# A fused recurrence and long convolution on one core: a list scheduler inside the kernel, the spectral sum on GpSimd, and the recurrence spread into the output stage

## The chip, the cores and the metric

One core of a Trainium2 chip. Times are device microseconds (us) of whole executions. "Span" is the profiled part of one execution, about 1.7 us less in each run here. PE is the tensor engine, PEld its weight loads, DVE the vector engine, ACT the scalar engine, POOL is GpSimd, SP the engine that issues loads and stores.

## The reference, cut to what matters

```python
# x, f_logit: (4, 6272, 256); four independent batches
f = lower_bound + (1 - lower_bound) * sigmoid(f_logit)
h[t] = f[t] * h[t-1] + (1 - f[t]) * x[t]          # recurrence over 6272 steps
x1, x2, x3 = split(h @ w_proj, 3)                  # 256 -> 768
conv = irfft(rfft(x2) * rfft(filter_fft))          # circular, length 6272
out = (x1 * conv * x3) @ w_out
```

Both kernels do the transform as matmuls (6272 = 49 x 128). Each batch passes through these stages: **recurrence** (transposes, a scan on DVE, gate products z = x1 x3), **projection and transform** of x2 (called P and f1), 16 **units** (forward transform, product with the filter's spectrum H, inverse transform), and **output** (last step of the inverse, product with z, projection with w_out).

## The kernel before

It weaves generators in program order. The recurrence of the next batch runs beside the units of this one; output, P and f1 follow alone.

```python
for b in range(B):
    mini(b)
    if b + 1 < B:
        weave((units(b), NU), (hgrn(b + 1), NCHK))
    else:
        run(units(b))
    if b + 1 < B:
        wraps()                    # copies of h that the projection of b+1 reads
    run(phase_o(b))
    if b + 1 < B:
        run(phase_p(b + 1)); run(phase_f1(b + 1))
```

A unit has two DVE products and, for each of four pairs, four inverse matmuls that also do the spectral sum in PSUM:

```python
for o, terms in (...):                                # two forward halves
    ...                                               # 2 matmuls each
    nc.vector.tensor_tensor(P[:TB, o, :, :, 1:64], px..., hh, op=AOP.mult)
for pr in range(UE // 2):
    for n, (a, h, v) in enumerate(((0, 0, VA), (0, 1, VB), (1, 0, VB), (1, 1, VN))):
        nc.tensor.matmul(o, P[:TB, a, h, 2*pr:2*pr+2, :], v[:TB], start=(n == 0), stop=(n == 3))
```

The output takes its PSUM pairs in turn from all eight banks (`pair()`), four pairs in rotation.

Of the kernel before, what the change touches and what calls it, by code (L numbers as in the profile page):

```python
# [9 lines left out]
F32 = mybir.dt.float32  # L10
# [11 lines left out]
S = 6272  # L22
# [4 lines left out]
CH = 512  # L27
NCHK = 13
# [20 lines left out]
def run(gen):  # L49
    for _ in gen:  # L50
        pass


def weave(*gens):

    lists = [(g, n) for g, n in gens]
    done = [0] * len(lists)
    total = sum(n for _, n in lists)
    for _ in range(total):
        k = min((i for i in range(len(lists)) if done[i] < lists[i][1]),  # L60
                key=lambda i: (done[i] + 1) / lists[i][1])
        next(lists[k][0])
        done[k] += 1
    for g, _ in lists:
        run(g)
# [3 lines left out]
def kernel(  # L69
# [13 lines left out]

    konst = ctx.enter_context(tc.tile_pool(name="konst", bufs=1))
    iden = konst.tile([128, 128], F32, name="iden")
    make_identity(nc, iden)
    pi_col = konst.tile([128, 1], F32, name="pi_col")
    nc.vector.memset(pi_col, math.pi)
# [7 lines left out]
    VN = konst.tile([128, 196], F16, name="VN")  # L96
# [9 lines left out]
    HB = (0, S + EW)  # L106

    raws = [HA[:, S + 4096 * k:S + 4096 * (k + 1)].bitcast(F32)
            .rearrange("m (r d) -> m r d", d=D) for k in range(3)]
    hws = [HA[:, S + 12288 + 1024 * k:S + 12288 + 1024 * (k + 1)]  # L110
           .rearrange("p (a n) -> p a n", a=2) for k in range(4)]

    hg = ctx.enter_context(tc.tile_pool(name="hg", bufs=2))
    dram = ctx.enter_context(tc.tile_pool(name="dram", bufs=1, space=bass.MemoryType.DRAM))
    H = [dram.tile([TB, 2, UE * 64], F16, name=f"H{u}") for u in range(NU)]
    zt = [konst.tile([128, 2, S], F16, name="z0"), None]
    psp = ctx.enter_context(tc.tile_pool(name="psp", bufs=1, space=PSUM))
    PS = psp.tile([128, 8, 512], F32, name="PS")
    turn = [0, 2]

    def pair():

        turn[0] = (turn[0] + 1) % turn[1]
        return PS[:, 2 * turn[0]:2 * turn[0] + 2]


    def hgrn(b):
        z = zt[b % 2]
        last = [None, None]
        for c in range(NCHK):  # L130
            t0 = c * CH
            nb = min(CH, S - t0) // 128
            n = nb * 128
            xt = hg.tile([128, 4, D], F32, name="xt", tag="xt", bufs=3)
            nc.sync.dma_start(xt[:, 0:nb], x[b, t0:t0 + n, :].rearrange("(j p) d -> p j d", p=128))
            ft = hg.tile([128, 4, D], F32, name="ft", tag="ft", bufs=3)
            nc.sync.dma_start(ft[:, 0:nb], f_logit[b, t0:t0 + n, :]
                              .rearrange("(j p) d -> p j d", p=128))
            nc.scalar.activation(ft[:, 0:nb], ft[:, 0:nb], AF.Sigmoid, scale=-1.0)  # L139
            nc.gpsimd.tensor_tensor(xt[:, 0:nb], xt[:, 0:nb], ft[:, 0:nb], op=AOP.mult)  # L140
            for kh in range(2):
                cols = slice(kh * 128, kh * 128 + 128)
                sT = PS[:, 6, 0:n]
                uT = PS[:, 7, 0:n]
                for j in range(nb):
                    nc.tensor.transpose(sT[:, j * 128:(j + 1) * 128], ft[:, j, cols], iden[:])  # L146
                for j in range(nb):
                    nc.tensor.transpose(uT[:, j * 128:(j + 1) * 128], xt[:, j, cols], iden[:])  # L148
                fT = hg.tile([128, CH], F32, name="fT", tag="fT")
                nc.scalar.activation(fT[:, 0:n], sT, AF.Identity,  # L150
                                     scale=nomc[:, kh:kh + 1], bias=1.0)
                h = hg.tile([128, CH], F32R, name="h", tag=f"h{kh}")
                nc.vector.tensor_tensor_scan(  # L153
                    h[:, 0:n], fT[:, 0:n], uT,
                    0.0 if c == 0 else last[kh][:, CH - 1:CH].bitcast(F32),
                    op0=AOP.mult, op1=AOP.add)
                last[kh] = h
                nc.gpsimd.tensor_copy(HA[:, HB[kh] + t0:HB[kh] + t0 + n],  # L158
                                      h[:, 0:n].bitcast(F32))
            for jb in range(2):  # L160
                for i in range(2):
                    js = slice(i * 256 + jb * 128, i * 256 + jb * 128 + 128)
                    for kh in range(2):
                        nc.tensor.matmul(PS[:, 4 + i, 0:n], W13[:, kh, js], last[kh][:, 0:n],  # L164
                                         start=(kh == 0), stop=(kh == 1))
                x1s = hg.tile([128, CH], F32, name="x1s", tag="x1s")
                nc.scalar.activation(x1s[:, 0:n], PS[:, 4, 0:n], AF.Copy, scale=ZS)  # L167
                nc.vector.tensor_tensor(z[:, jb, t0:t0 + n], PS[:, 5, 0:n], x1s[:, 0:n],  # L168
                                        op=AOP.mult)
            yield  # L170

    def wraps():
        for a, z in ((0, 2048), (2048, 4096), (4096, E0)):
            nc.sync.dma_start(HA[:, S + a:S + z], HA[:, a:z])
        for a, z in ((128, 2048), (2048, 4096), (4096, S)):
            nc.sync.dma_start(HA[:, HB[1] - S + a:HB[1] - S + z], HA[:, HB[1] + a:HB[1] + z])


    def prepare(tmp):
        wcol = tmp.tile([128, 2], F32, name="wcol")  # L180
        nc.sync.dma_start(wcol, lower_bound.rearrange("(a p) -> p a", p=128))
        nc.vector.tensor_scalar(omc[:], in0=wcol[:], scalar1=-1.0, scalar2=1.0,
                                op0=AOP.mult, op1=AOP.add)
        nc.vector.tensor_scalar(nomc[:], in0=wcol[:], scalar1=1.0, scalar2=-1.0,
                                op0=AOP.mult, op1=AOP.add)


        wp = raws[0][:, 0:6].rearrange("p a d -> p (a d)").rearrange("p (k j) -> p k j", k=2)
        nc.sync.dma_start(wp, moe_w_proj.rearrange("(a p) j -> p a j", p=128))
        wo = raws[1][:, 0:2]  # L190
        nc.sync.dma_start(wo, moe_w_out.rearrange("(a p) j -> p a j", p=128))
        for kh in range(2):
            nc.vector.tensor_scalar(wp[:, kh, :], in0=wp[:, kh, :], scalar1=omc[:, kh:kh + 1],
                                    scalar2=None, op0=AOP.mult)
            for i, j0 in enumerate((0, 512)):
                dst = slice(i * 256, (i + 1) * 256)
                nc.vector.tensor_copy(W13[:, kh, dst], wp[:, kh, j0:j0 + 256])
            for p in range(2):
                nc.vector.tensor_copy(
                    W2[:, kh].rearrange("k (g p e) -> k p e g", p=2, e=2)[:, p],  # L200
                    wp[:, kh, 256 + p * 128:256 + (p + 1) * 128]
                    .rearrange("k (e g) -> k e g", e=2))
        nc.vector.tensor_copy(Woh[:], wo[:])
        nc.vector.tensor_tensor(Wol[:], wo[:], Woh[:], op=AOP.subtract)
        yield
        def icol(pattern, base, cm, n, name):
            ti = tmp.tile([128, n], I32, name=name + "_i", tag="icol_i")
            nc.gpsimd.iota(ti[:], pattern=pattern, base=base, channel_multiplier=cm)
            tf = tmp.tile([128, n], F32, name=name + "_f", tag="tf" if n > 1 else name,
                          bufs=2 if n > 1 else 1)  # L210
            nc.vector.tensor_copy(tf[:], ti[:])
            return tf

        def trig(P, n, cval, pval, off, den, name, offcol=None):

            v = tmp.tile([128, n], F32, name="tv", tag="tv")
            if offcol is not None:
                nc.vector.tensor_scalar(v[:P], in0=cval[:P], scalar1=pval[:P],
                                        scalar2=offcol[:P], op0=AOP.mult, op1=AOP.add)
            elif isinstance(off, (int, float)):  # L220
                nc.vector.tensor_scalar(v[:P], in0=cval[:P], scalar1=pval[:P],
                                        scalar2=float(off), op0=AOP.mult, op1=AOP.add)
            else:
                nc.vector.scalar_tensor_tensor(v[:P], in0=cval[:P], scalar=pval[:P],
                                               in1=off[:P], op0=AOP.mult, op1=AOP.add)
            qi = tmp.tile([128, n], I32, name="tqi", tag="tqi")
            nc.vector.tensor_scalar(qi[:P], in0=v[:P], scalar1=1.0 / den, scalar2=None,
                                    op0=AOP.mult)
            qf = tmp.tile([128, n], F32, name="tqf", tag="tqf")
# [315 lines left out]
```

## Time and profile before

755.77 us, median of 3 runs (753.34 to 756.71). The prediction shows the page and the windows on round limits. For the comparison, here is the second round again, cut exactly where PE starts a stage (units with recurrence, output, P and f1). The columns are the window and its length; busy time and instructions of PE, PEld, DVE, ACT, POOL; the granted PE clock; DMA share; GB/s.

Two of them, from the timeline of DVE in that round (start, length, line, operation, and in brackets the idle time before it and what ended it):

```profile
347.13 0.69 DVE L168 TENSOR_TENSOR z<-PS,x1s 128x512 f16<-128x512 f32 x1 [1.08 <-ACT x1s L167]
348.83 0.69 DVE L168 TENSOR_TENSOR z<-PS,x1s 128x512 f16<-128x512 f32 x1 [1.00 <-PE PS L164]
```

DVE stands at the head of its fixed order waiting for a gate's operands. No product of a unit was ready to fill the gaps either: PE, in its own fixed order, issued the next unit's forward matmuls (line 435) only at 349.82.

### The profile page before, as it was taken

How to read it: one execution, taken by the hardware profiler on the slowest of the kernel's cores; microseconds unless marked ns; L12 is line 12 of the kernel's file. 1: busy time of each engine (PE TensorE's matmuls, PEld its weight loads, DVE VectorE, ACT ScalarE, POOL GpSimd, SP SyncE). 2: the span in 40 equal slices, each digit the busy share in tenths (PEclk: the TensorE clock that was granted, in tenths of full speed). 3: DMA queues.
4: the chain of work that ended last, by engine and by line, in shares of the span. 5: the costliest groups of instructions: out<-in, count | busy, mean ns of one | idle time of the engine just before them, and what ended most of it. 6: DMA issues, size and time to landing. Idle time of an engine off the chain costs nothing.

```text
span 751.1 us, 13229 instructions
## 1 busy us (share of the span) xinstructions
PE 650.6 (87%) x5252; PEld 503.8 (67%) x5252; DVE 514.1 (68%) x574; ACT 390.4 (52%) x495; POOL 197.6 (26%) x264
## 2 busy tenths in 40 slices
PE   4699887589999979988989979989999899889897
PEld 3577665486666668876656668966666588857686
DVE  6996554179888853388878854498888844778732
ACT  3697765475555533474456543575555423823233
POOL 2445433302454340002454430004454100001000
PEclk9999999789999989999999999999999999979999
DMA  9755546403656454404646464305646234112144
GB/s 327 259 182 190 184 123 195 156 1 110 193 161 219 154 191 168 176 2 142 192 143 223 150 205 179 140 5 180 201 153 204 88 143 181 52 33 76 44 169 176
DMA packets 73630, 113.99 MB, mean 152 GB/s; under 512 B 4416, under 2 KB 55488, under 8 KB 72800
## 3 DMA queue, kind: packets, MB, share of 16 engines
q1 hardware_dynamic: 73568, 113.15, 44.8%
q8 instruction: 41, 0.67, 0.4%
q14 instruction: 21, 0.17, 0.1%
HBM read 71.70 MB, written 28.90 MB: 134 GB/s over the span
## 4 chain that ended last, share of the span: by engine, by line
PE 45%; DVE 24%; issue 11%; ACT 10%; DMA 9%; POOL 1%; DVEq 0%; SPq 0%; ACTq 0%
PE PS L481 11%; PE PS L164 9%; DVE h L153 8%; PE PS L447 5%; PE PS L379 5%; DMA ft<-in_f_logit_dram 5%; DVE PP L439 4%; DVE PP L473 4%; PE PS L468 3%; PE PS L148 2%; DMA Hu<-H 2%; PE PS L435 2%; PE PS L346 2%; PE PS L394 2%; ACT x1s L167 2%
## 5 line engine op out<-in xcount | busy, mean ns | idle before, releaser
L164 PE MATMUL PS<-h,W 128*128 128x512 f32 (+1 forms) x416 | 148.5, 441 | 16.6 <-DVE h L153 10.1
L439 DVE TENSOR_TENSOR PP<-PS,Hu 98x1008 f16<-98x1008 f32 x128 | 151.3, 1193 | 9.8 <-PE PS L435 4.3
L140 POOL TENSOR_TENSOR xt<-xt,ft 128x1024 f32<-128x1024 f32 (+1 forms) x52 | 116.3, 2238 | 103.2 <-DMA xt<-in_x_dram 49.2
L153 DVE TENSOR_TENSOR_SCAN h<-fT,h,PS 128x512 fp32r<-128x512 f32 (+1 forms) x96 | 115.9, 1208 | 20.5 <-ACT fT L150 7.8
L473 DVE TENSOR_TENSOR PP<-PS,z 128x1024 f16<-128x1024 f32 (+1 forms) x52 | 59.5, 1182 | 91.8 <-PE PS L468 76.6
L168 DVE TENSOR_TENSOR z<-PS,x1s 128x512 f16<-128x512 f32 (+1 forms) x104 | 68.4, 658 | 67.4 <-ACT x1s L167 39.9
L447 PEld LDWEIGHTS <-PP 98*128 98x128 f16 x1024 | 86.4, 100 | 40.9 <-issue 29.5
L158 POOL CAST HA<-h 128x512 f16<-128x512 f32 (+1 forms) x104 | 61.3, 592 | 171.8 <-DVE h L153 167.1
L485 ACT ACTIVATE osb<-PS 128x1024 f32<-128x1024 f32 (+1 forms) x52 | 50.8, 977 | 101.8 <-PE PS L481 100.8
L481 PE MATMUL PS<-Woh,PP 128*128 128x256 f16 x392 | 87.9, 275 | 11.8 <-DVE PP L473 11.4
L447 PE MATMUL PS<-VB,PP 98*128 98x196 f16 x512 | 97.7, 254 | 0.4 <-DVE PP L439 0.3
L481 PEld LDWEIGHTS <-PP 128*128 128x128 f16 x784 | 83.4, 114 | 19.7 <-DVE PP L473 18.4
L167 ACT ACTIVATE x1s<-PS 128x512 f32<-128x512 f32 (+1 forms) x104 | 59.4, 572 | 69.6 <-PE PS L164 68.7
L164 PEld LDWEIGHTS PS<-h,W 128*128 128x128 f32 x416 | 65.9, 195 | 43.2 <-DVE h L153 23.8
L450 ACT CAST Th<-PS 128x784 f16<-128x784 f32 x64 | 51.9, 811 | 72.0 <-PE PS L447 71.9
L481 PE MATMUL PS<-Wol,PP 128*128 128x256 f16 x392 | 87.2, 273 | 0.0
L150 ACT ACTIVATE fT<-PS,nomc 128x512 f32<-128x512 f32 (+1 forms) x104 | 68.9, 662 | 30.5 <-PE PS L146 25.7
L435 PE MATMUL PS<-HA,FT 98*128 98x512 f16 x256 | 78.0, 388 | 4.8 <-DVE PP L439 3.0
L148 PE MATMUL PS<-iden,xt 128*128 128x128 f32 x392 | 68.0, 281 | 12.0 <-DVE h L153 11.0
L146 PE MATMUL PS<-iden,ft 128*128 128x128 f32 x392 | 69.3, 278 | 3.4 <-ACT fT L150 2.8
L139 ACT ACTIVATE ft<-ft 128x1024 f32<-128x1024 f32 (+1 forms) x52 | 52.4, 1007 | 33.0 <-DMA ft<-in_f_logit_dram 32.7
L148 PEld LDWEIGHTS PS<-iden,xt 128*128 128x128 f32 x392 | 46.2, 142 | 30.4 <-DVE h L153 24.2
(112 smaller groups left out, 843.3 us busy)
## 6 DMA issues: line engine op xcount, KB each, us to landing
xt<-in_x_dram SPq DMA_DIRECT2D x48, 512.0 KB
ft<-in_f_logit_dram SPq DMA_DIRECT2D x48, 512.0 KB
out_dram<-osb SPq DMA_DIRECT2D x48, 512.0 KB
Hu<-H SPq DMA_DIRECT2D x64, 196.0 KB
HA<-in_moe_filter_fft_dram SPq DMA_DIRECT2D x6, 1024.0 KB
HA<-HA SPq DMA_DIRECT2D x12, 512.0 KB
H<-HA SPq DMA_DIRECT2D x16, 196.0 KB
HA<-HA SPq DMA_DIRECT2D x4, 544.0 KB
```

What stands on the lines that cost most here:

```text
L140: nc.gpsimd.tensor_tensor(xt[:, 0:nb], xt[:, 0:nb], ft[:, 0:nb], op=AOP.mult)
L146: nc.tensor.transpose(sT[:, j * 128:(j + 1) * 128], ft[:, j, cols], iden[:])
L148: nc.tensor.transpose(uT[:, j * 128:(j + 1) * 128], xt[:, j, cols], iden[:])
L150: nc.scalar.activation(fT[:, 0:n], sT, AF.Identity, scale=nomc[:, kh:kh + 1], bias=1.0)
L153: nc.vector.tensor_tensor_scan(h[:, 0:n], fT[:, 0:n], uT, 0.0 if c == 0 else last[kh][:, CH - 1:CH].bitcast(F32), op0=AOP.mult, op1=AOP.add)
L164: nc.tensor.matmul(PS[:, 4 + i, 0:n], W13[:, kh, js], last[kh][:, 0:n], start=(kh == 0), stop=(kh == 1))
L167: nc.scalar.activation(x1s[:, 0:n], PS[:, 4, 0:n], AF.Copy, scale=ZS)
L435: nc.tensor.matmul(PS[:, o, :], FT[:TB, tb, :], A[:TB, es, r, :], start=(n == 0), stop=(n == 1))
L439: nc.vector.tensor_tensor(P[:TB, o, :, :, 1:64], px.unsqueeze(1).broadcast_to([TB, 2, UE, 63]), hh, op=AOP.mult)
L447: nc.tensor.matmul(o, P[:TB, a, h, 2 * pr:2 * pr + 2, :], v[:TB], start=(n == 0), stop=(n == 3))
L473: nc.vector.tensor_tensor(y, pc[:, :, 0:rn * 128].rearrange("p a (m i) -> p a m i", i=rn), z[:, :, :, r0:r0 + rn], op=AOP.mult)
L481: nc.tensor.matmul(po[:, i, :], y[:, kh, :, i], w[:, kh, :], start=(n == 0), stop=(n == 3))
```

## The change

The intent: let a scheduler with modelled durations choose the order on every engine for all batches together, take half of the inverse matmuls off PE, and let the recurrence run on into the output stage, where DVE is idle. Every operation is recorded with cost, reads and writes; `emit` then places them one by one, each time the candidate that can start first, ties to the longest remaining chain ("level").

```diff
+class Plan:
+    def op(self, cost, fn, r=(), w=(), kb=0.0, table=None): ...   # records, finds predecessors
+    def emit(self):
+        for i in reversed(todo):
+            o["level"] = c + max((ops[j]["level"] for j in o["succ"]), default=0.0)
+        while cand:
+            ...                        # per engine: key = (earliest start, -level, i)
+            o["end"] = self.free[e] = at + o["cost"][e]
+            o["fn"](e)
 ...
-            for n, (a, h, v) in enumerate(((0, 0, VA), (0, 1, VB), (1, 0, VB), (1, 1, VN))):
+            op({"POOL": 2.2}, lambda e, k=k: nc.gpsimd.tensor_tensor(      # the spectral sum
+                Y[:TB, k, :, :, 1:64], PP[:TB, k, 0, :, :, 1:64], PP[:TB, k, 1, :, :, 1:64],
+                op=AOP.add), r=[("P", k, 0), ("P", k, 1)], w=[("Y", k)])
+            op({"POOL": 0.28}, ... Y[:TB, k, :, :, 0] <- zm ..., r=["zm"], w=[("Y", k, 0)])
+            ...                        # two inverse matmuls per pair instead of four
 ...
+            cb, ob = (4 * (g % 2), 4 * (g % 2) + 2) if b == B - 1 else (0, 2)   # output's banks
 ...
+            prepare(tmp)
+            hgrn(0)
+            plan.emit()                # first list: constants, filter, recurrence of batch 0
+        ...
+        wraps(); phase_p(0); phase_f1(0); mini(0)
+        for b in range(B):
+            units(b)
+            phase_o(b)
+            if b + 1 < B:
+                hgrn(b + 1); wraps(); phase_p(b + 1); phase_f1(b + 1); mini(b + 1)
+        plan.emit()                    # second list: everything else
```

Further: copies may go to either ACT or DVE, a third (negated) plane of H is stored and loaded, input buffers fall from three to two, and output keeps to PSUM banks 0 to 3 except in the last batch, as the recurrence holds 4 to 7.

## The prediction

> **What bounds the kernel now.** I read the page first (busy shares, slices, groups), then the table of windows, then the timeline inside two stages. The chain of waits only confirmed the stages.
>
> ```profile
> PE 650.6 (87%) x5252; PEld 503.8 (67%) x5252; DVE 514.1 (68%) x574; ACT 390.4 (52%) x495; POOL 197.6 (26%) x264
> PE   4699887589999979988989979989999899889897
> DVE  6996554179888853388878854498888844778732
> POOL 2445433302454340002454430004454100001000
> L439 DVE TENSOR_TENSOR PP<-PS,Hu 98x1008 f16<-98x1008 f32 x128 | 151.3, 1193 | 9.8 <-PE PS L435 4.3
> L140 POOL TENSOR_TENSOR xt<-xt,ft 128x1024 f32<-128x1024 f32 (+1 forms) x52 | 116.3, 2238 | 103.2 <-DMA xt<-in_x_dram 49.2
> L153 DVE TENSOR_TENSOR_SCAN h<-fT,h,PS 128x512 fp32r<-128x512 f32 (+1 forms) x96 | 115.9, 1208 | 20.5 <-ACT fT L150 7.8
> ```
>
> No engine is full on average; DVE and POOL swing by stage. The windows give the stages (length, then busy time of PE, PE weight loads, DVE, ACT, POOL):
>
> ```profile
> 75.00:147.00 72.00, 56.23 (x334) 42.08 (x332) 32.09 (x36) 45.35 (x66) 26.70 (x38) 0.95 0.52 163
> ...
> 503.00:603.00 100.00, 91.01 (x642) 63.28 (x642) 83.89 (x89) 51.96 (x78) 39.61 (x52) 1.00 0.50 162
> 603.00:638.00 35.00, 32.25 (x368) 29.30 (x364) 13.91 (x13) 11.53 (x12) 0.25 (x1) 1.00 0.38 153
> 638.00:661.00 23.00, 20.70 (x234) 18.61 (x233) 18.39 (x16) 18.79 (x17) 0.00 (x0) 1.00 0.13 51
> 661.00:706.00 45.00, 41.29 (x299) 28.82 (x300) 38.05 (x37) 11.37 (x14) 3.94 (x16) 0.89 0.22 63
> 706.00:751.00 45.00, 36.10 (x414) 32.40 (x411) 15.64 (x14) 14.33 (x15) 0.00 (x0) 1.00 0.35 144
> ```
>
> So: a head to 147 us (constants, filter spectrum, recurrence of batch 0); about 27 us of first projection and transform; then three rounds of about 162 us, each made of **units plus the next recurrence** (100: DVE 84%), **output** (35 to 38: PE, with DVE at 40%) and **projection and transform** (23 to 24: DVE and ACT at 80%); then units alone (45) and output alone (45). Neighbouring stages have different limits: that is the room for the change.
>
> PE's busy time is inflated, as its instructions overlap. In the timeline they start at a fixed pitch:
>
> ```profile
> 690.42 0.33 PE L447 MATMUL PS<-VB,PP 98*128 98x196 f16 x2
> 690.59 0.25 PE L447 MATMUL PS<-VN,PP 98*128 98x196 f16 x1
> 690.67 0.25 PE L447 MATMUL PS<-VA,PP 98*128 98x196 f16 x1
> ...
> 718.71 0.27 PE L481 MATMUL PS<-Woh,PP 128*128 128x256 f16 x1
> 718.81 0.27 PE L481 MATMUL PS<-Wol,PP 128*128 128x256 f16 x1
> ```
>
> That is 0.083 us for 196 columns (a duration of 0.25) and 0.109 for 256. Read the same way: 512 columns 0.21 (line 435) and 0.27 (line 164), a transpose 0.11, line 468 about 0.055. PE's work in a round's units stage is then 21.6 transposes + 27 gates + 13.4 forward + 21.2 inverse (256 x 0.083) = 83 of 100 us: DVE and PE are both about 83% there and alternate through single PSUM banks. The output stage holds 10.8 + 21.4 = 32 us of PE.
>
> **What the Trainium skill says.** "Perfetto Trace Analysis", Optimization Strategy: where the most-contended engine changes between regimes, interleave the regimes. The windows agree (DVE 84% then 40%). "TensorE: Matmul & The Clock Gate", Back-to-back issue gap: N/2.4 + 2.5 ns for one isolated stream, 84 and 109 ns at 196 and 256 columns; the pitches above agree, with weight loads hidden. "GPSIMD Engine Reference", 3.1: a two-input add costs about 2.6 cycles an element at 1.2 GHz; 1024 elements would be 2.2 us, and line 140's full form shows 2.36, so it agrees. "SBUF — State Buffer", Who interferes with whom: DVE and GpSimd block each other when DVE has two SBUF inputs or a 2-port mode. The trace agrees for small SBUF-only DVE operations in the head (line 233 of 98x98 means 887 ns, against 220 for a 128x128 one). But scan, products, gate and output product each take one operand from PSUM, so more GpSimd work should not slow them.
>
> **The change, part by part.**
>
> *Spectral sum on GpSimd.* A third, negated filter plane is stored, so both products of a unit can be added before the inverse matmuls. These fall from 1024 to 512: 128 x 0.083 = 10.6 us of PE in each batch, 42 in all. Added: 64 GpSimd adds of 98x1008, estimated from line 140 at 2364 x 1008/1024 = 2.33 us, 149 us in all; GpSimd goes from 198 to about 347 us. The 128 DVE products stay. The sum also lengthens each unit's chain by a 2.3 us step, with two buffers. Filter loads grow by half (196 to 294 KB, 64 of them), about 6 MB on 114, with DMA half busy: hidden.
>
> *Recurrence spread.* Units (b), output (b) and recurrence (b+1) share one span; units and output keep PSUM banks 0 to 3, the recurrence banks 4 to 7. Work in it per round:
> - PE: 83 - 10.6 + 32 = 105 us.
> - DVE: scans 31.4, gate products 17.1, spectral products 37.6, output products 14.9, plus one or two copies: 102 us.
> - GpSimd: 16 x (2.33 + 0.26) = 41, recurrence 28.4 + 15.3 = 44: 85 us.
> - ACT: about 71 us.
>
> Before, this work took 100 + 37 = 137 to 140. It cannot go below 105. The listing of the changed order, without times, puts 2 of a round's 26 scans into the transform stage, 7 beside the units and 17 from there into the output. Beside the units: DVE 37.6 + 7 x 1.27 + 7 x 0.69 + 2 for the mini transform = 53 to 55; GpSimd 41 + about 12.6 = 54. With hand-over waits I take 59. In the output part: PE 32 + 17/26 x 48.6 = 64; over 0.95 that is 67. Sum **126 us**, chosen near the 83% that the old stage reaches (105/0.83 = 126). The wraps of the last chunk now follow a recurrence that ends near the end of the output: 1 to 2 us exposed.
>
> *Projection and transform.* Same copies over two engines: 23 to 24 us, scans now inside it. Round: 126 + 1 + 23.5 = **150.5** against 162.
>
> *Head.* All of it is ordered by the scheduler. It removes the alternation between sine and sigmoid tables (12 loads of 1.28 us become 4), adds the negated plane (16 copies of 512), and has two input buffers instead of three. PE work there is about 48.6 + 21 (rotation, line 321) + 33 (lines 334, 346) = 103 of 147 us, so there is slack; but one chunk's buffer lives about 11 us (load 4.5, sigmoid 1.3, product 2.6, transposes and one scan 2.7), so two buffers cannot go under 5.5 us a chunk, 72 in all. I take **132** against 147; this is a choice.
>
> *Tail.* Units alone have all eight banks, but DVE needs 38 and GpSimd 41: 44 against 45. Output alone has alternating banks, so the next inverse no longer waits behind a 1.2 us product: 13 x 2.7 = 35 of PE, plus start and the final store: 40 against 45.
>
> Sum: 132 + 26 + 3 x 150.5 + 84 = 693.5 us of span; the execution reads some 2 to 5 us over the span (752.78 against 751.1; median 755.77). I trim a little because units can begin as soon as their part of the transform is done: **690 us**, 8.7% less.
>
> **The rivals.**
> *A, near-perfect packing.* A list order with every buffer known in advance keeps PE full: 112 a round and 120 for the head. For it: two engines with nearly equal sums, and waits now are short. Against: single banks for both recurrence operands (transpose, ACT, scan) and two banks for each of the other steps. About 640 us.
> *B, GpSimd becomes the bound of the units.* If the 16-bit add over runs of 63 takes 3 us instead of 2.33, units take 16 x 3.3 + 12.6 = 65 plus waits, in all four batches. For it: 54 us of GpSimd equals DVE's share already, and each sum sits on the unit's chain. Against: line 140 does more in 2.36. About 725 us.
> *C, the fixed order goes stale.* The order comes from modelled durations. If loads land later than modelled, in-order engines stall behind one wait; with two input buffers and one queue for loads, filters and stores, each chunk could wait 1 us: +13 a round and in the head, about 740. For it: loads already end many waits (the input load 49.2 us before line 140). Against: chunks come every 9 to 10 us now instead of 7.5.
> *D, no gain, as the saved PE time was hidden.* True of the PE part alone (DVE led the units), but the output stage has 60% of DVE free, which the trace shows directly.
>
> **Range and chances.** The middle is the sum above; A and half of B or C give 640 to 735, and I take 645 to 732 for 8 in 10. Under 740.7 is faster by over 2%: B alone keeps that, B with C does not. Faster 0.93, same 0.05, slower 0.02.
>
> **What would show it.** The inverse matmuls 512 at an unchanged pitch; the GpSimd add at 2.2 to 2.4 us and line 439's successor still near 1.19 us; in each round DVE at 80% or more throughout units and output; the output part longer than before (60 to 70 us) and PE-led; 12 table loads down to 4; the head under 140. I am wrong if the adds exceed 2.8 us, if loads end waits in every chunk, if the head does not shrink, or if PE idles over 20% in the output part.

## More of the kernel before

```profile
336.70:442.20 105.50, 92.72 (x618) 63.05 (x617) 84.34 (x87) 54.04 (x80) 44.32 (x54) 0.98 0.56 176
442.20:479.30 37.10, 34.33 (x393) 31.11 (x394) 14.72 (x14) 11.86 (x14) 2.60 (x2) 1.00 0.42 163
479.30:501.40 22.10, 19.82 (x230) 18.42 (x231) 17.45 (x16) 18.33 (x17) 0.00 (x0) 1.00 0.14 55
```

The thing to see is the first line: DVE works 84.3 of 105.5 us, so 21 us of a stage that has enough work for it are lost to waits.

## The result, and the profile after

After: 728.33 us median (725.46 to 730.72, 4 runs); before in the same rounds: 754.56 (751.54 to 756.71). Ratio 0.9654, 95% interval 0.9603 to 0.9704. Ratios here and below are the mean time of one kernel's runs over that of the kernel before in the same rounds, so not quite the ratio of the medians. The gain is 3.5% against 8.7% predicted; 728 lies inside the range, 38 us above its middle.

The page of the changed kernel (busy row, DVE and clock in 40 slices, three groups):

```profile
PE 611.6 (85%) x4740; PEld 474.1 (65%) x4740; DVE 510.6 (71%) x577; ACT 385.8 (53%) x495; POOL 327.0 (45%) x325
...
DVE  6834886169899666688997665888976666976342
...
PEclk9798999689799999998999999979999999978699
...
L608 DVE TENSOR_TENSOR PP<-PS,Hu 98x1008 f16<-98x1008 f32 x128 | 147.4, 1199 | 28.8 <-POOL Y L613 14.4
L613 POOL TENSOR_TENSOR Y<-PP 98x1008 f16<-98x1008 f16 x64 | 133.9, 2100 | 74.8 <-DVE PP L608 51.9
...
L258 DVE TENSOR_TENSOR_SCAN hs<-fTs,hs,PS 128x512 fp32r<-128x512 f32 (+1 forms) x96 | 115.9, 1207 | 22.8 <-PE PS L244 12.7
```

The sum takes 2.10 us and the products are as quick as before (1.199 against 1.193 us), but half of the products' idle time now ends on the sum, line 613. DVE swings less: within the rounds it no longer falls to 3 or 4 tenths; it does so only in the head, in a stall after it, and at the very end.

Windows of the stall after the head (first line), of the second round (three lines, cut as before), of the last units and of the last output:

```profile
131.00:146.00 15.00, 1.19 (x7) 0.72 (x8) 0.32 (x2) 2.11 (x2) 4.68 (x2) 0.52 0.94 309
...
320.90:384.10 63.20, 51.37 (x313) 32.68 (x312) 56.54 (x57) 28.50 (x40) 51.65 (x47) 0.95 0.54 163
384.10:442.40 58.30, 58.26 (x535) 48.13 (x533) 37.97 (x40) 31.82 (x45) 22.59 (x22) 1.00 0.74 251
442.40:472.10 29.70, 25.74 (x270) 23.46 (x268) 21.72 (x21) 23.51 (x25) 5.12 (x5) 0.94 0.25 82
622.00:679.00 57.00, 38.59 (x193) 22.93 (x191) 40.64 (x37) 12.06 (x16) 35.87 (x32) 0.75 0.25 75
679.00:724.00 45.00, 36.29 (x392) 32.53 (x392) 15.38 (x14) 13.04 (x13) 0.00 (x0) 0.92 0.36 144
```

In the output part (second of the three lines) PE is now busy throughout with DVE at 65%; beside the units (first of them) DVE reaches 89%. The weak places are the first line and the last two: 15 us in which hardly any engine works (GpSimd 4.7 us, the others about 2 or less) and DMA is at 94%, and last units in which neither DVE (71%) nor POOL (63%) is full and the clock granted to PE is 0.75.

By stages, from PE's timeline (one profile each). "Round" is the mean of the three distances between starts of units, "last output" ends with the span. The head ends here with the last gate product; in the kernel before, filter work went on until about 145.6, which is why the prediction, cutting at 147, has 27 us where this table has 33.9.

| us | end of head | head to first units | round | last units | last output | span |
|---|---|---|---|---|---|---|
| before | 140.9 | 33.9 | 161.6 | 50.1 | 41.3 | 751.1 |
| predicted | 132 | 26 | 150.5 | 44 | 40 | 693.5 |
| after | 131.3 | 40.6 | 149.9 | 58.3 | 44.0 | 723.8 |

So head and rounds came as predicted, and 30 us of span were missed in two places: 14.6 us between head and first units, and 18.3 us in the tail (14.3 and 4.0).

### The profile page after: what moved, and what is told of

It reads as the page before. It is cut to its first block, busy times and chain, and to the rows that moved or that the text cites. A ratio compares the mean times of both kernels' runs of the same rounds, so it can differ in the third digit from the quotient of the medians.

```text
span 723.8 us, 12254 instructions
## 1 busy us (share of the span) xinstructions
PE 611.6 (85%) x4740; PEld 474.1 (65%) x4740; DVE 510.6 (71%) x577; ACT 385.8 (53%) x495; POOL 327.0 (45%) x325
## 5 line engine op out<-in xcount | busy, mean ns | idle before, releaser
L608 DVE TENSOR_TENSOR PP<-PS,Hu 98x1008 f16<-98x1008 f32 x128 | 147.4, 1199 | 28.8 <-POOL Y L613 14.4
L613 POOL TENSOR_TENSOR Y<-PP 98x1008 f16<-98x1008 f16 x64 | 133.9, 2100 | 74.8 <-DVE PP L608 51.9
L235 POOL TENSOR_TENSOR XT<-XT,FL 128x1024 f32<-128x1024 f32 (+1 forms) x52 | 116.7, 2245 | 86.9 <-DMA XT<-in_x_dram 47.8
L201 ACT CAST X<-PS 128x784 f16<-128x784 f32 (+2 forms) x89 | 89.0, 1009 | 99.4 <-PE PS L624 82.2
L269 PE MATMUL PS<-hs,W 128*128 128x512 f32 (+1 forms) x416 | 132.1, 422 | 6.5 <-ACT HA L201 2.8
L261 POOL CAST HA<-hs 128x512 f16<-128x512 f32 (+1 forms) x104 | 60.5, 590 | 158.9 <-DVE hs L258 154.2
L258 DVE TENSOR_TENSOR_SCAN hs<-fTs,hs,PS 128x512 fp32r<-128x512 f32 (+1 forms) x96 | 115.9, 1207 | 22.8 <-PE PS L244 12.7
L254 ACT ACTIVATE fTs<-PS,nomc 128x512 f32<-128x512 f32 (+1 forms) x104 | 69.3, 666 | 53.6 <-DVE hs L258 26.2
L269 PEld LDWEIGHTS PS<-hs,W 128*128 128x128 f32 x416 | 68.8, 193 | 23.6 <-DVE z L280 6.0
L244 PE MATMUL PS<-iden,XT 128*128 128x128 f32 x392 | 66.0, 290 | 12.3 <-DVE hs L258 11.2
L233 ACT ACTIVATE FL<-FL 128x1024 f32<-128x1024 f32 (+1 forms) x52 | 52.4, 1010 | 44.5 <-DMA FL<-in_f_logit_dram 44.2
L244 PE MATMUL PS<-iden,FL 128*128 128x128 f32 x392 | 65.4, 289 | 10.0 <-ACT FL L233 6.2
L601 PEld LDWEIGHTS <-FT 98*128 98x128 f16 x256 | 25.5, 105 | 67.6 <-issue 60.0
```

Source lines behind the costliest of these rows:

```text
L201: nc.scalar.copy(dst, src)
L235: op({"POOL": 0.1 + 0.535 * nb}, lambda e, xt=xt, ft=ft: nc.gpsimd.tensor_tensor(xt, xt, ft, op=AOP.mult), r=[("ft", k)], w=[("xt", k)])
L244: nc.tensor.transpose(dst[:, j * 128:(j + 1) * 128], src[:, j, cols], iden[:])
L254: nc.scalar.activation(fT, sT, AF.Identity, scale=nomc[:, kh:kh + 1], bias=1.0), r=bank(6), w=[("fT", j)])
L258: nc.vector.tensor_tensor_scan(h, fT, uT, init, op0=AOP.mult, op1=AOP.add),
L269: nc.tensor.matmul(PS[:, 4 + i, 0:n], W13[:, kh, js], hs[:, kh, hk, 0:n], start=(kh == 0), stop=(kh == 1))
```

## The experiments

Seventeen runs, put together by question (the letters e to i give the order of the calls). Each is one edit of the changed kernel unless it says otherwise; a table with all stages stands at the end of the section.

### The two misses

The timelines gave a cause for each. The wraps of batch 0 are recorded after the first `emit`, so they leave late and among loads of the next batch. SP's issues of wraps (the first four and the last three of eight; between these two lines stand one more wrap, two loads of Hu and four loads of the next batch's input):

```profile
126.53 3.30 SPq L288 DMA_DIRECT2D HA<-HA  x4
...
134.75 3.37 SPq L288 DMA_DIRECT2D HA<-HA  x3
```

and PE's projection, line 540, with the wait in brackets:

```profile
133.71 0.40 PE L540 MATMUL PS<-W,HA 128*128 128x256 f16 x1 [2.15 <-DMA HA<-HA]
145.77 11.98 PE L540 MATMUL PS<-W,HA 128*128 128x256 f16 x95 [11.66 <-DMA HA<-HA]
```

In the last units GpSimd's order is sum, sum, copy, copy: the 0.26 us copy of a unit's column zero stands behind the next unit's 2.1 us sum, so inverse matmuls start a sum late, and the next pair of sums waits for them in turn, at about 6 us per two units:

```profile
642.09 4.55 DVE L608 TENSOR_TENSOR PP<-PS,Hu 98x1008 f16<-98x1008 f32 x4 [0.84 <-POOL Y L613]
643.35 0.74 PE L601 MATMUL PS<-HA,FT 98*128 98x512 f16 x2 [1.46 <-DVE PP L608]
644.05 0.39 POOL L616 COPY Y<-zm 98x16 f16<-98x16 f16 x2
644.36 0.35 PE L624 MATMUL PS<-VA,Y 98*128 98x196 f16 x1 [0.27 <-POOL Y L616]
644.50 0.37 PE L624 MATMUL PS<-VB,Y 98*128 98x196 f16 x1
...
645.99 4.15 POOL L613 TENSOR_TENSOR Y<-PP 98x1008 f16<-98x1008 f16 x2 [1.55 <-PE PS L624]
```

The inverse matmuls of that burst follow at 0.165 us instead of 0.083. One more loss stands in the trace before it: at 628.45 a small DVE addition with two SBUF inputs (line 584) took 2.16 us instead of 0.43, while a GpSimd sum of 2.09 us ran from 628.24. It stands inside the longest wait of PE in this stage, 4.25 us until 632.11.

**e1_wraps_first.** The wraps go into the first list.

```diff
             hgrn(0)
+            wraps()
             plan.emit()
 ...
-        wraps()
         phase_p(0)
```

> The eight wrap copies of batch 0 are put into the scheduler's first list, before the barrier between the two lists, so that they go out as the recurrence of batch 0 delivers. Theory (the wraps were left out of the first list and stand in the queue behind and among 2.6 MB of prefetch): the 14.7 us between the last gate matmul of the head (131.1 us) and the first dense projection matmul (145.8 us) falls to 3 to 6 us; total 716 to 721 us. Rival (the transfers must be made anyway and the queue is full there, so the wait only moves): head or first units grow by as much, total 725 to 729 us.

710.83 us (707.75 to 714.18), ratio 0.9444 [0.9381, 0.9508]. From the last gate to the end of the projection: 12.2 us against 26.5. The projection now runs in one piece:

```profile
130.21 12.42 PE L540 MATMUL PS<-W,HA 128*128 128x256 f16 x98
```

The stall was the wraps, and it is all gone: more than expected.

**e2_copy_first.** The sum of the next unit waits for this unit's column copy, which puts the copy ahead of it (in the list's record of reads; the sum does not read it).

```diff
-                op=AOP.add), r=[("P", k, 0), ("P", k, 1)], w=[("Y", k)])
+                op=AOP.add), r=[("P", k, 0), ("P", k, 1), ("Y", 1 - k, 0)], w=[("Y", k)])
```

> Each GpSimd sum is made to wait for the previous unit's 0.26 us zero-column copy, so a copy no longer stands behind the next 2.1 us sum; nothing else is changed. Theory (order on GpSimd starts the inverse matmuls one sum too late, and the next sum waits for them through the two buffers): the last units, 58 us, fall to 44 to 48 us, the units of the three rounds lose 1 to 4 us each, clock of the last units above 0.9; total 706 to 716 us. Rival (the sum itself is the bound, or the low clock comes from elsewhere): last units stay at 55 us or more, total 725 to 729 us.

713.65 us (711.85 to 715.81), ratio 0.9482 [0.9429, 0.9535]. The last units fall from 58.3 to 49.4, short of the 44 to 48 expected; so the order was a part of that miss, not the whole. Two more parts of the expectation failed: the rounds stayed (149.4 against 149.9), and the clock granted in the last units was 0.84, not above 0.9.

**e3_tail_order.** In the last batch, a group's projection is recorded after the next group's inverse, so that PE has work while DVE makes the product.

```diff
-               w=bank(cb, cb + 1))
+               w=bank(cb, cb + 1) + [("inv", g % 2)])
 ...
+            # last batch: projection and store of group g also read ("inv", (g + 1) % 2)
```

> In the last batch's output the projection of group g is made to wait for the inverse matmuls of group g+1 on the same engine, so PE has work while DVE multiplies. Theory (the list order issues two projections, one inverse, then waits 1.3 us for DVE, as the kernel before did): last output 44.6 us falls to 38 to 40 us; total 721 to 724 us. Rival (stores or ACT set the pace there): unchanged, 727 to 729 us.

725.54 us (720.99 to 729.59), ratio 0.9626 [0.9548, 0.9705]: the last output falls from 44.0 to 41.2 (38 to 40 was expected), but the total cannot be told from the changed kernel's.

**e4_all_three.** The three edits together.

> All three edits together. Theory: the gains add, as they lie one after the other in time: 14.7 to 5, 58 to 46, 44.6 to 39 and a few us in the rounds, total 690 to 704 us, which is the sum that the prediction had. Rival (one shared cause, such as the low clock or the DMA queue): the gains overlap, total 708 us or more.

696.15 us (695.65 to 699.56), ratio 0.9258 [0.9207, 0.9309], better than both kernels. The three gains (0.9654 less 0.9444, 0.9482, 0.9626) add up to 0.041, some 31 us, and 0.040 came. Still the last units take 50.8 and the tail 92.6, no less than the 91.4 before.

**f3_hold.** Is it the barrier that delays the wraps, or the loads among them? Here the wraps stay in the second list, but the first three chunks of loads of batch 1 and the first two of Hu wait for them.

```diff
-                   w=[t], kb=n)
+                   r=["wrapped"] if b == 1 and c < 3 else [], w=[t], kb=n)
 ...
-               r=[("H", u)], w=[("Hu", k)], kb=300)
+               r=[("H", u)] + (["wrapped"] if b == 0 and u < 2 else []), w=[("Hu", k)], kb=300)
```

> The changed kernel with the first batch's wraps still in the second list, but the next batch's first input loads and the first two loads of Hu held until the wraps have been issued. Tells the prefetch in the queue from the barrier itself. If the prefetch ahead of the wraps makes the stall: from the end of the gate matmuls to the dense projection 14.7 falls to about 7, the whole to about 720. If the late issue behind the barrier makes it: stays at 14, the whole 727 to 730. (With the wraps in the first list it was about 1 and 711.)

720.12 us (716.17 to 723.19), ratio 0.9504 [0.9449, 0.9558]. The dense projection begins 6.5 us after the last gate (133.2 to 139.7) instead of 14.5, as the first theory expected, and ends 19.9 us after it. Of the loss between 26.5 and 12.2, then, about half is the loads that share the queue; the other half, by subtraction, is the late issue behind the barrier. The issues agree: the last wrap leaves SP 6.2 us after the last gate in the changed kernel, 1.9 after it here, and 3.6 before it in e1.

### What the sum is worth

**f1_no_sum.** Four inverse matmuls per pair again, no GpSimd sum, in all batches.

```diff
-            op({"POOL": 2.2}, ... nc.gpsimd.tensor_tensor(Y..., PP..., PP..., op=AOP.add) ...)
-                    for n, v in enumerate((VA, VB)):
-                        nc.tensor.matmul(o, Y[:TB, k, n, 2 * pr:2 * pr + 2, :], v[:TB], ...)
+                    for n in range(4):
+                        nc.tensor.matmul(o, PP[:TB, k, n // 2, n % 2, 2 * pr:2 * pr + 2, :],
+                                         (VA, VB)[n % 2][:TB], start=(n == 0), stop=(n == 3))
```

> The changed kernel with the spectral sum taken back: four inverse matmuls per pair on the tensor engine instead of two and a GpSimd sum, in every batch. Value of the sum. Theory (the units part is bound by the vector engine and by the stalls around GpSimd, and the saved matmuls were mostly hidden): each round stays at 150 (147 to 153), the last units fall from 58 to about 49, the whole 715 to 722. Rival (the tensor engine binds the rounds): each round grows by about 11 to 13 to 161 to 163, the whole is then about 728 + 3 x 12 - 9 = 755.

702.05 us (701.17 to 705.9), ratio 0.9285 [0.9229, 0.9341]; repeated later as i0_no_sum_again: 704.76, ratio 0.9358. Both theories missed: **without the sum the kernel is 22 to 28 us faster** (0.030 to 0.037 of 755). Rounds fall from 149.9 to 145.5 and the last units from 58.3 to 50.8, though PE does 512 matmuls more. The units part of its second round:

```profile
317.00:378.90 61.90, 56.80 (x435) 43.27 (x434) 54.42 (x55) 28.97 (x39) 19.22 (x30) 0.97 0.57 173
```

DVE is at 88% there, as with the sum (89%): DVE led this part all along. (This is the round that gained least; in the other two the units part fell from 63.1 and 66.8 to 57.1 and 56.0 us.) The PE time saved by the sum was time in which PE would have waited for DVE.

> The kernel without the sum, unchanged, beside the run with all banks on the same chip, so that the two are compared directly. Both theories expect what it gave before: rounds of 145 to 147, ratio to the kernel before 0.923 to 0.934, about 702.

**f4_best.** e4, with the sums of the last batch alone taken back.

> All three repairs together, and the last batch's sums done by the tensor engine with four inverse matmuls, as in the kernel before. In the last units nothing else fills the tensor engine, and GpSimd's 2.1 us sum per pair of units is longer than what it saves. Theory: last units 50.8 falls to about 45, the whole 696 to about 690. Rival (the last units are bound by the vector engine's products at 38 to 45 whatever the sums): unchanged at 50 and 696.

702.02 us (697.93 to 703.43), ratio 0.9259 [0.9209, 0.9309]: no gain over e4's 0.9258. The last units took 53.7. So after the copy's order is mended, something other than the sum holds the last units at 50. The products' waits there point to it: in e4 5.2 us of them end on loads of Hu and 0.3 on the sum. h4 below tests it, in the kernel without the sum.

**g4_small_sum.** All orders unchanged, but the sum adds 8 of 63 columns. Its output is wrong, which doesn't matter for the time.

```diff
-                Y[:TB, k, :, :, 1:64], PP[:TB, k, 0, :, :, 1:64], PP[:TB, k, 1, :, :, 1:64],
+                Y[:TB, k, :, :, 1:9], PP[:TB, k, 0, :, :, 1:9], PP[:TB, k, 1, :, :, 1:9],
```

> The changed kernel with every engine's order unchanged, but each GpSimd sum adds 8 of its 63 columns (98x128 elements instead of 98x1008; the result is wrong on purpose). Takes away the duration of the sum[...], keeps the extra step and the 512 inverse matmuls. Theory (the sum's 2.1 us of GpSimd time in the units part is the cost: GpSimd was busy 47 of 57 us there, late sums hold up the inverse matmuls): each round falls from 150 to 141 to 146, the last units from 58 to about 45 to 49, the whole to 685 to 705. Rival (the additional hop from vector engine to GpSimd to tensor engine is the cost): rounds stay at 149 to 151, last units 55 to 58, the whole 720 to 730.

718.34 us (714.72 to 723.47), ratio 0.9495 [0.9434, 0.9555]. The sum took 0.459 us, the last units fell to 49.2, but the rounds stayed at 151.8. (The profile is of the slowest of the four executions, 723.47 us; but the gain by the ratio, 0.016 or 12 us, is not much more than the 9.1 us of the last units either.) My theory held for the tail only: in the rounds the duration of the sum is not what costs.

**h1_small_replan.** The small sum again (wrong result), now with its planned cost lowered to 0.46, so that the list is made anew.

```diff
-            op({"POOL": 2.2}, lambda e, k=k: nc.gpsimd.tensor_tensor(
+            op({"POOL": 0.46}, lambda e, k=k: nc.gpsimd.tensor_tensor(
```

> The changed kernel with the small sum (8 of 63 columns, wrong result on purpose), and the planned cost of the sum lowered from 2.2 to 0.46 us, which is what it took, so that the scheduler orders everything anew. If the order made for a 2.2 us sum is what costs 4 to 6 us per round: rounds fall from 151.8 (small sum, old order) to 144 to 147, the whole to about 695 to 700. If the additional hop itself costs it: rounds stay at 149 to 152 and the whole at 714 to 722.

706.35 us (705.14 to 711.8), ratio 0.9385 [0.9336, 0.9434], rounds 147.4. By the ratios the new plan gained 0.011, some 8 us. So an order made for a 2.2 us sum was a part of the loss; how large a part in the rounds stays open, as g4's 151.8 is from a slow execution. What the extra hand-over itself costs is not told apart from zero by these runs (0.9385 against 0.9285 and 0.9358).

**h2_idle_sum.** f1, plus a full-size GpSimd addition per unit whose result nobody reads.

```diff
+                op({"POOL": 2.2}, lambda e, k=k: nc.gpsimd.tensor_tensor(
+                    Y[:TB, k, :, :, 1:64], Y[:TB, k, :, :, 1:64], Y[:TB, 1 - k, :, :, 1:64],
+                    op=AOP.add), r=[("P", k, 0), ("P", k, 1)], w=[("Y", k)])
```

> The kernel without the sum (four inverse matmuls), plus a GpSimd addition of full size per unit whose result nobody reads. Adds the sum's load alone, no wait on it by the tensor engine. If the load on GpSimd[...] costs the time: rounds rise from 145.5 to 149 to 151, last units above 55, the whole 720 to 730. If only the wait behind it costs: rounds 144 to 147, last units 49 to 52, the whole 699 to 706.

714.59 us (710.12 to 717.25), ratio 0.9473 [0.9414, 0.9532], rounds 147.8, last units 53.5: between the two theories. An addition on GpSimd whose result nobody reads costs 9 to 14 us (0.0115 to 0.019 of 755). DVE's products did not slow (1.197 and 1.198 us). Its small addition with two SBUF inputs, once held up in the changed kernel (mean 860 ns: three of about 425 and the one of 2164 shown above), took 425 ns each time here, but none of the four met a GpSimd instruction, so that is no test. I put the loss down to places in GpSimd's queue, where the column copies and the recurrence's casts stand behind additions; that is argued from the order, not shown by a run of its own. A rival stands untested: the edit records the idle addition as a reader of the products' buffer, so the list, though not the chip, holds the next products for it and makes a different order.

### What the spreading is worth

**f2_not_spread.** The recurrence of b+1 must end before the output of b begins.

```diff
             units(b)
-            phase_o(b)
             if b + 1 < B:
                 hgrn(b + 1)
+            phase_o(b)
 ...
-            op({"PE": 0.235 * rn}, inv, r=[("Th", u) for u in range(NU)] + ["Th"],
+            op({"PE": 0.235 * rn}, inv, r=[("Th", u) for u in range(NU)] + ["Th"]
+               + [("z", (b + 1) % 2, jb, NCHK - 1) for jb in range(2) if b + 1 < B],
```

> The changed kernel, but the recurrence of the next batch has to finish before the output of this batch begins, as in the kernel before. Value of the spreading. Theory: this is where the gain per round comes from, so each round goes back to 160 to 162, the whole to 758 to 765. Rival (the gain per round comes from the order the list scheduler gives, whatever the recurrence does): rounds unchanged at 150, the whole 725 to 732.

764.18 us, ratio 1.0103, and a **wrong result**: the tiles of projection and inverse share one buffer, and nothing recorded that the projection of b+1 must wait for the output's reads of it. By the list, the changed kernel is right only because its projection also waits for a recurrence that ends late. A hand-made list of dependencies can be incomplete and still work until the order shifts.

**g1_not_spread.** The same with that dependency recorded.

```diff
-                .rearrange("m r e -> m e r")), r=bank(pb, pb + 1) + ["Th"], w=[("x2", g)])
+                .rearrange("m r e -> m e r")), r=bank(pb, pb + 1) + ["Th"],
+               w=[("x2", g), ("Tr", g)])
 # and every inverse of the output reads ("Tr", 0..12)
```

> The run without spreading, mended: the projection's copies now wait for the output part that still reads the same buffer, a dependency that the list did not have. Otherwise as before: the recurrence of the next batch ends before the output begins. The wrong one took 764 with rounds of about 162. Expect 160 to 166 per round and 762 to 775; correct. If it comes near 730 the earlier figure was an effect of the wrong order.

776.34 us (769.84 to 779.32), ratio 1.0244 [1.0188, 1.03] (whether slower by 2% is unclear), correct, rounds 167.0, both a little above what was expected. The time of the wrong run was thus no artefact of its wrong order.

**g2_neither.** The same without the sum: only the list scheduler is left.

> No sum and no spreading (mended): what the list scheduler alone does. Theory (nearly the whole gain per round is the spreading, and the sum costs something in each round): rounds of 156 to 162, that is close to the 161.6 of the kernel before, the whole 740 to 755. Rival (the scheduler's order has a gain of its own, whatever is spread): rounds of 148 to 153, the whole 705 to 725.

759.73 us (757.82 to 762.44), ratio 1.0042 [0.9999, 1.0085], rounds 160.8 as the theory said (the whole a little above it). It looked as though spreading were the whole gain. But the output part of its second round was far longer than before's 37.1:

```profile
424.70:478.00 53.30, 37.44 (x406) 31.43 (x406) 15.77 (x15) 12.84 (x15) 2.60 (x2) 1.00 0.31 121
```

PE waits 1.32 to 1.38 us for DVE's product in ten of the 13 groups. The output of all but the last batch keeps to four banks, made for a recurrence that runs beside it; in this run there was none.

**i1_all_banks.** g2 with all eight banks for every output.

```diff
-            cb, ob = (4 * (g % 2), 4 * (g % 2) + 2) if b == B - 1 else (0, 2)
+            cb, ob = 4 * (g % 2), 4 * (g % 2) + 2
```

> No sum and no spreading, but the output part of every batch alternates between all eight PSUM banks, as the kernel before does, where the run with neither used only four and its tensor engine waited 1.3 us for the vector engine in each of 13 groups. Rival that this run is to test (the list scheduler alone has the gain, and the loss without spreading is only the handicap of four banks): the output part falls from 53 to about 37, rounds from 160.8 to 144 to 148, the whole to 700 to 716, so spreading itself is worth nothing. Theory (spreading is worth something beyond that): rounds stay above 152, the whole above 730.

708.65 us (706.57 to 714.95), ratio 0.9414 [0.9355, 0.9472], rounds 145.0; on the same chip f1, which spreads, gave 0.9358 [0.9305, 0.9411]. The intervals overlap; f1's first measurement, on another chip, was 0.9285 [0.9229, 0.9341], clear of i1's. **My theory falls: by the ratios spreading the recurrence into the output is worth 4 to 10 us (0.0056 to 0.013), on the same chip nothing that these runs can tell,** and none of it in the rounds (145.0 against 145.5 and 144.1); what differs is the stretch from head to first units, 48.9 against 41.2 and 42.3. This holds without the sum; no run has the sum, no spreading and eight banks. The gain per round comes with the scheduler's order:

```profile
325.50:403.50 78.00, 75.16 (x555) 56.89 (x554) 74.21 (x80) 45.18 (x67) 36.98 (x47) 1.00 0.70 227
403.50:442.00 38.50, 34.82 (x385) 30.99 (x385) 15.14 (x14) 12.50 (x13) 2.59 (x2) 0.96 0.42 166
442.00:473.90 31.90, 29.68 (x307) 27.04 (x305) 24.23 (x22) 27.49 (x30) 7.72 (x7) 1.00 0.31 104
```

Against the three lines of the kernel before: DVE's idle time beside the units fell from 21.2 to 3.8 us, and 10 us of its work left that stage; the transform stage, where scans now run too, has 6.8 us more of DVE's work and grew by 9.8; the output is about as long. Net 16 us. That it is the order is by exclusion: i1 also has the third plane of H and two input buffers instead of three, which take resources and give none, wraps in eight pieces instead of six, and the free choice of engine for copies, which changed little (DVE made 24 of the copies into X, 29 into A and 4 of the output, against 24, 32 and 0 before). Where the kernel before showed two waits of 1 us, DVE's timeline (lines 258 scan, 609 product, 280 gate product) has none:

```profile
346.93 1.27 DVE L258 TENSOR_TENSOR_SCAN hs<-fTs,hs,PS 128x512 fp32r<-128x512 f32 x1
348.12 1.18 DVE L609 TENSOR_TENSOR PP<-PS,Hu 98x1008 f16<-98x1008 f32 x1
349.21 0.68 DVE L280 TENSOR_TENSOR z<-PS,x1s 128x512 f16<-128x512 f32 x1
```

### The best version

**g3_best.** f1 with e1's wraps and e3's last output.

> The version that the runs point to: no spectral sum, the first batch's wraps in the first list, the last output's projections one group late. Adding up: 702 for no sum, less about 15 for the wraps, less 2 to 3 for the last output: 682 to 688. Rival: part of the wraps' gain came from somewhere the missing sum has already emptied; then 690 to 696, no better than the three repairs with the sum (696).

692.51 us (686.75 to 694.45), ratio 0.9136 [0.9086, 0.9186]: in medians the rival's range, by the ratio 11 to 17 us better than f1. The last units still take 49.9.

**h4_three_hu.** g3 with three buffers for Hu.

```diff
-        Hu = cv.tile([128, 2, 3, UE * 64], F16, name="Hu")
+        Hu = cv.tile([128, 3, 3, UE * 64], F16, name="Hu")
 # load and products use u % 3; the unused Y is dropped
```

> The best version so far (no sum, wraps first, last output one group late: 692) with three buffers for Hu instead of two. In its last units the vector engine works 40 of 50 us and waits mostly for the Hu loads, which start only when a buffer comes free. If those loads bound the last units: 49.9 falls to 43 to 46, and the units parts of the rounds by 2 to 4 each, the whole 677 to 686. If the double-buffered products (tensor engine and vector engine taking turns) bound them: unchanged, 689 to 694.

685.53 us (683.23 to 686.15), ratio 0.9089 [0.9053, 0.9125], the best of all by the ratio, though its interval overlaps that of g3, measured on another chip. The last units fall to 43.9. DVE in the last units of f1 (two buffers, first two lines) and of this run:

```profile
622.28 4.55 DVE L608 TENSOR_TENSOR PP<-PS,Hu 98x1008 f16<-98x1008 f32 x4 [0.78 <-DMA Hu<-H]
627.69 4.55 DVE L608 TENSOR_TENSOR PP<-PS,Hu 98x1008 f16<-98x1008 f32 x4 [0.86 <-DMA Hu<-H]
```

```profile
615.38 11.23 DVE L608 TENSOR_TENSOR PP<-PS,Hu 98x1008 f16<-98x1008 f32 x10 [0.39 <-PE PS L640]
626.94 15.69 DVE L608 TENSOR_TENSOR PP<-PS,Hu 98x1008 f16<-98x1008 f32 x14 [0.32 <-DMA Hu<-H]
```

Four products and a wait for a load became fourteen in a row. Only the tail gained, not the rounds (146.3 and 147.4), against the expectation of 2 to 4 us each, although the products' waits for Hu in the rounds fell from 15.6 us in g3 to 0.3.

| us, one profile each | end of head | head to first units | round | last units | last output | ratio to before |
|---|---|---|---|---|---|---|
| after | 131.3 | 40.6 | 149.9 | 58.3 | 44.0 | 0.9654 |
| e1 wraps first | 130.4 | 26.6 | 149.8 | 56.6 | 43.1 | 0.9444 |
| e2 copy first | 127.5 | 41.3 | 149.4 | 49.4 | 44.1 | 0.9482 |
| e3 last output | 131.7 | 40.8 | 151.0 | 59.5 | 41.2 | 0.9626 |
| e4 all three | 130.7 | 27.7 | 147.7 | 50.8 | 41.8 | 0.9258 |
| f3 loads held | 133.2 | 36.2 | 148.7 | 58.8 | 43.4 | 0.9504 |
| f1 no sum | 128.8 | 41.2 | 145.5 | 50.8 | 42.2 | 0.9285 |
| i0 no sum again | 130.2 | 42.3 | 144.1 | 51.5 | 43.1 | 0.9358 |
| f4 e4, sum not in last batch | 130.5 | 25.5 | 150.3 | 53.7 | 40.4 | 0.9259 |
| g4 small sum | 129.8 | 42.7 | 151.8 | 49.2 | 44.6 | 0.9495 |
| h1 small sum, planned anew | 127.1 | 43.2 | 147.4 | 47.1 | 43.7 | 0.9385 |
| h2 idle sum | 130.6 | 40.8 | 147.8 | 53.5 | 44.3 | 0.9473 |
| f2 not spread (wrong) | 128.5 | 47.1 | 160.9 | 59.2 | 44.5 | 1.0103 |
| g1 not spread | 130.5 | 45.4 | 167.0 | 57.7 | 43.1 | 1.0244 |
| g2 neither | 130.9 | 49.3 | 160.8 | 51.2 | 43.7 | 1.0042 |
| i1 neither, all banks | 128.7 | 48.9 | 145.0 | 50.0 | 42.2 | 0.9414 |
| g3 no sum, wraps, last output | 133.3 | 26.7 | 146.3 | 49.9 | 40.4 | 0.9136 |
| h4 g3, three Hu | 132.9 | 25.9 | 147.4 | 43.9 | 39.5 | 0.9089 |

Kernels of equal design differ by up to 3 us in a round from profile to profile (e4, f4), so a single difference of 2 us in that column says nothing.

## Why the prediction was right or wrong

- **Head 132.** Right: 131.3.
- **"26 us of first projection and transform", "wraps 1 to 2 us exposed".** This failed for the first batch: 40.6 us. I took the transition from the kernel before, though the diff shows a new list boundary between recurrence and wraps. e1 gives 26.6 with the wraps ahead of the boundary, so the term was right for a kernel that the change did not make. The step that failed is the wait for the wraps: the 26 us carried over hold one of 4.67 us (PE in the kernel before, until 150.58), and here PE waited 2.15 and 11.66 us for them.
- **Round 150.5.** The number was right (149.9), its derivation was not, and that it came out is luck. In the second round units, output with wraps, and projection with transform took 63.2, 58.3 and 29.7 us against 59, 68 and 23.5 predicted: 4 and 6 too long, 10 too short. It took 10.6 us per batch off PE for the sum and held PE to 83% of the merged span. Runs show the sum's saving is worth less than nothing (145.5 and 144.1 without it), and that spreading isn't needed for the rest (145.0 without either, with eight banks). The part of the gain that is real, DVE's waits beside the units falling from 21.2 to 3.8 us, stood in the window tables that I read, as 84% of DVE, and I took it as a bound rather than as slack that a better order can use.
- **Tail: "DVE needs 38 and GpSimd 41: 44".** This failed: 58.3. I took the largest sum of work over the stage and left the chain out: product, sum, column copy behind the next sum, inverse, with two buffers. e2 shows the order's share (49.4 with the copy first), h4 that of the buffers: 44 was the right figure for DVE-led units, reached without the sum and with a third Hu buffer (43.9). No run has the sum with three buffers. Last output 40 against 44.0: a smaller miss of the same kind, PE's order; 39.5 and 40.4 with it mended.
- **Costs of single operations.** Right: sum 2.10 us (2.33 estimated), products unchanged, inverse pitch unchanged where PE was kept fed. Wrong: the larger filter loads were not hidden; the products' waits for Hu rose from 2.4 to 11.2 us.
- **Three readings that do not hold as they stand.** The 887 ns of line 233 are the mean of 211, 213 and 2236; the long one ran during a GpSimd product of 2381 ns, so the blocking was there, in one of three. The formula for the pitch is given by the Trainium skill, "TensorE: Matmul & The Clock Gate", Back-to-back issue gap, for one isolated matmul, not for a stream; the page says it is off for a stream with weight loads, yet the pitches here (0.083 and 0.109 us, with a weight load to each matmul) came out by it. And the execution reads 1.7 us over the span, not 2 to 5.
- **The rivals.** A did not come. B did not come by its mechanism, as GpSimd is 45% busy over the span and its sum was quicker than estimated; yet the sum cost 22 to 28 us, a part of it through the order (h1). C is right in kind: a wrong order and late loads, though for wraps and Hu, not for the input chunks. D I dismissed on account of the output stage; for the sum it happened, and more, as the kernel is 22 to 28 us faster without it.
- **The signs I named.** None of the signs for a wrong prediction came up (sum under 2.8 us, head shorter, PE full in the output part, and loads ended the GpSimd product's wait in 19 of 52 chunks, as before). One sign of a right one failed: DVE was to be at 80% throughout, and was at 65% in the output part. They all watched the steady rounds; both misses lay at the ends, where nothing else fills the engines.

The total: 693.5 us of predicted span, less 0.7 (head), plus 14.6 (first projection), less 1.9 (rounds), plus 18.3 (tail) is 723.8. The execution that was profiled took 725.46; the median, 728.33, is of all four.

## What to carry to other kernels

Taking work off an engine pays only in the stage where that engine ends the waits; here half of the inverse matmuls were taken off PE in a stage led by DVE, and the detour through GpSimd cost 22 to 28 us. When a large change bundles several ideas, undo each alone and look for handicaps that belong to the bundle (here four PSUM banks) before crediting one of them. With a list scheduler, inspect list boundaries, the order of short operations behind long ones on one queue, and the last batch, since these are where both misses lay here.

## What the Trainium skill lacked or had wrong

- "Perfetto Trace Analysis", Optimization Strategy, says that interleaving regimes with different contended engines may help, besides optimizing within each. It lacks a caution on which to do first: here interleaving was worth nothing that could be told on one chip (0.9358 with, 0.9414 without, overlapping intervals; 0.9285 with on another) once order within the regimes was good; DVE's idle time beside the units fell from 21.2 to 3.8 us without it.
- "GPSIMD Engine Reference", 3.1, gives about 2.6 cycles an element for a two-input add. Close, but it is one number: the 16-bit sums took 2100 ns for 1008 elements a partition and 459 ns for 128. A line through these two points, an estimate, is 1.87 ns an element, 2.24 cycles at the page's 1.2 GHz, plus about 220 ns fixed, for which that section has no figure.
- "TensorE: Matmul & The Clock Gate", Why this matters for your kernels, warns of PE-idle gaps above about 3 us. In the last units of the changed kernel the pitch doubled from 0.083 to 0.165 us both after a gap of 4.25 us and after one of 1.46 us (ends of matmuls are modelled), and the clock granted over that stage was 0.75. Yet ten gaps of 1.32 to 1.38 us in g2's output left the clock at 1.00: the length of one gap alone does not decide.
- No page that I read has the cost of a short operation behind a long one on an in-order queue: moving a 0.26 us copy ahead of a 2.1 us sum gained 13 us (0.9654 to 0.9482).
